# Later stores and a per-head copy: two small changes to a fused attention and MLP kernel

## The chip, the cores and the metric

The kernel runs on one core of a Trainium2 chip. The metric is the device time of one execution in microseconds, the median of several runs; lower is better. A profile of one execution goes with it: for every engine the instructions with start and duration, and for each wait what ended it. TensorE is called PE in the profile (PEld is its loading of weights), VectorE DVE, ScalarE ACT, GpSimd POOL, and the queue that issues most transfers SPq.

## The reference

Inputs are q, k, v of 8 batches, 8 heads, 576 positions and 64 columns in fp32, and the weights of an MLP (512 to 2048 to 512). Attention is of the Nyström kind: queries and keys are averaged over segments of 18 positions to 32 landmarks, three softmax matrices are made, and the inverse of the middle one is found by six Newton steps.

```python
A  = sm(q, k_lm)        # 576 x 32
Bm = sm(q_lm, k_lm)     # 32 x 32
C  = sm(q_lm, k)        # 32 x 576
Z = Bm.T / (norm1(Bm) * norminf(Bm) + 1e-6)
for _ in range(6):
    Z = 2 * Z - Z @ Bm @ Z
x = (A @ Z @ C @ v)     # then heads side by side: 8 x 576 x 512
# MLP
xn = (x - mean) / sqrt(var + 1e-6) * g_ln
out = x + relu(xn @ w_ch1) @ w_ch2
```

## The kernel before

The kernel interleaves two streams in one program. The attention works on sets of batches: (0), (1), (2), (3, 4), (5, 6), (7). A unit is half a batch, that is four heads whose 32 landmarks fill the 128 partitions; a set has W = 2 or 4 units. The MLP works on blocks of 128 rows, four blocks to a group, and is cut into small pieces (a generator) that fill TensorE while the attention waits for other engines. `fill(n)` takes n pieces. The order of instructions on each engine is thus fixed when the program is made.

In a Newton step the four heads of a unit are multiplied at once: `ebd` holds the four 32 x 32 matrices on the diagonal of a 128 x 128 operand, with zeros elsewhere. Before the change it is a product of the matrix, read four times over, with a mask of zeros and ones. The first set (batch 0) doesn't use it.

```python
def diagonal(name, src, W, mask):
    t = asm.tile([P, W, 4, LM], FP16, name=name, tag=name, bufs=1)
    dve.tensor_tensor(out=t[:], in0=src[:, :, None, :].broadcast_to([P, W, 4, LM]),
                      in1=mask, op=ALU.mult)
    return t

# one Newton step (attention2)
for it in range(6):
    psn = p1([P, W, LM + D], "psn")
    for w in range(W):
        MM(psn[:, w, lo:], ebd[:, w, :, :].rearrange("p a l -> p (a l)"), st[:, w, lo:])
    dve.scalar_tensor_tensor(out=stn[:, :, lo:], in0=st[:, :, lo:], scalar=2.0,
                             in1=psn[:, :, lo:], op0=ALU.mult, op1=ALU.subtract)
    st = stn
    if it < 5:
        ebd = diagonal("ebd", st[:, :, 0:LM], W, masks(W))
    else:
        bmbd = diagonal("bmbd", bm16, W, maskw...)
    ...   # scores of the queries in the first W // 2 steps
    yield
```

Beside this, GpSimd casts the incoming q, k and v to fp16 (`nat`, `natv`) and sums segments (`asum`, `s`); VectorE transposes them (`xT`), normalizes the attention's output into rows (`xblk`), and adds the MLP's result to them (`ot`). A finished block is centered (`xn`, mostly on GpSimd) and turned by a transposing transfer (`xnT`), which the MLP's first product `psh` reads. All of these transfers, the loads and the stores go through one queue, in order.

```python
def turn_by_dma(j):
    keep(nc.sync.dma_start(out=xnTs[g][:, :, ts(u, P)], in_=xn_of.pop(j)[:],
                           transpose=True))

# end of an MLP block
ot = mout.tile([P, DM], FP32, name="ot", tag="ot")          # 4 buffers
dve.scalar_tensor_tensor(out=ot[:], in0=pso[:], scalar=rstds[g][:, u:u + 1],
                         in1=x_blk.pop(j)[:], op0=ALU.mult, op1=ALU.add)
store(j, ot)                                                # two transfers
yield True

# the loop over an attention set
for step, _ in enumerate(attention2(c.bs, c)):
    fill(count[step])
    settle()              # centers finished blocks and issues their turns
    ...                   # next_cast, next_load, next_job
```

Of the kernel before, what the change touches and what calls it, by code (L numbers as in the profile page):

```python
# [9 lines left out]
FP16 = mybir.dt.float16  # L10
# [3 lines left out]
ALU = mybir.AluOpType  # L14
AX = mybir.AxisListType

P = 128
# [3 lines left out]
def kernel(  # L21
# [10 lines left out]
    nc = tc.nc  # L32
# [6 lines left out]
    LM = 32  # L39
# [12 lines left out]
        name=nc.get_next_instruction_name(), act_func_set_id=6, ins=[], outs=[]))  # L52

    const = ctx.enter_context(tc.tile_pool(name="const", bufs=1))
# [15 lines left out]
    dve, pool, scalar = Ordered(nc.vector), Ordered(nc.gpsimd), Ordered(nc.scalar)  # L70
# [75 lines left out]
    mask4 = const.tile([P, 4], FP32, name="mask4")  # L146
# [16 lines left out]


    maskw = const.tile([P, 4, 4], FP16, name="maskw")
    mask16 = const.tile([P, 4], FP16, name="mask16")
    nc.gpsimd.tensor_copy(out=mask16[:], in_=mask4[:])
    for w in range(4):
        nc.gpsimd.tensor_copy(out=maskw[:, w, :], in_=(mask4t if w % 2 else mask4)[:])

# [7 lines left out]
    for i in range(NV):  # L178
        t = const.tile([P, H // 2, NJ, D + 1], FP16, name=f"natv{i}")
# [3 lines left out]
    for i in range(NZ):  # L183
        t = const.tile([P, 4, D + 1], FP16, name=f"zcbd{i}")
# [77 lines left out]
    asm = ctx.enter_context(tc.tile_pool(name="asm", bufs=2))  # L262
# [16 lines left out]
            MM(idle[:, 0:cols], zeros[:], zeros[:, None, :].broadcast_to([P, cols // P, P]))  # L279


    def diagonal(name, src, W, mask):
        t = asm.tile([P, W, 4, LM], FP16, name=name, tag=name, bufs=1)
        dve.tensor_tensor(out=t[:], in0=src[:, :, None, :].broadcast_to([P, W, 4, LM]),
                          in1=mask, op=ALU.mult)
        return t

    def masks(W):
        return mask16[:, None, :, None].broadcast_to([P, W, 4, LM])


    def attention(bs):
        units = [(b, u) for b in bs for u in range(U)]
        W = len(units)
# [11 lines left out]
        for w, (b, u) in enumerate(units):  # L306
            for i, nm in enumerate(("q", "k")):
# [13 lines left out]
                t = aprep.tile([P, NJ, P], FP16, name="xT", tag="xT" + nm, bufs=5 if nm == "q" else 4)  # L321
# [14 lines left out]
            out=qbd[:],  # L336
            in0=pss[:, 0, :, :].rearrange("p u (e l) -> p (u e) l", e=2)[:, :, None, :]
            .broadcast_to([P, W * 2, 2, LM]),
            in1=mask2[:, None, :, None].broadcast_to([P, W * 2, 2, LM]), op=ALU.mult)
# [16 lines left out]
        bm16 = asm.tile([P, W, LM], FP16, name="bm16", tag="bm16")  # L356
# [22 lines left out]
        for w in range(W):  # L379
            for h in range(4):  # L380
# [4 lines left out]
                                op=ALU.max)  # L385
# [6 lines left out]
                                in1=cinv[:, :, None].broadcast_to([P, W, LM]),  # L392
                                op=ALU.mult)
        if not first:
            ebd = diagonal("ebd", st[:, :, 0:LM], W, masks(W))


        v_used.update(bs)
# [18 lines left out]
        for it in range(6):  # L417
            lo = 0 if it < 5 else LM
            psn = p1([P, W, LM + D], "psn")
            for w in range(W):  # L420
                if first:
                    for h in range(4):
                        sl = ds(32 * h, 32)
                        MM(psn[sl, w, lo:], st[sl, w, 0:LM], st[sl, w, lo:],
                           rb=32 * h, cb=32 * h)
                else:
                    MM(psn[:, w, lo:], ebd[:, w, :, :].rearrange("p a l -> p (a l)"),
                       st[:, w, lo:])
            stn = asm.tile([P, W, LM + D], FP16, name="st", tag="st")
            dve.scalar_tensor_tensor(out=stn[:, :, lo:], in0=st[:, :, lo:], scalar=2.0,  # L430
                                           in1=psn[:, :, lo:], op0=ALU.mult,
                                           op1=ALU.subtract)
            st = stn
            if not first and it < 5:
                ebd = diagonal("ebd", st[:, :, 0:LM], W, masks(W))
            if it < W:
                w = it
                psa = p2([P, NJ, 64], FP32, "psa")
                for (j0, j1) in ((0, 8), (8, NJ)):
                    for h in range(4):  # L440
                        r, e = divmod(h, 2)
                        rows = ds(64 * r, 64)
                        MM(psa[ds(32 * h, 32), j0:j1, :], klm[rows, w, ds(32 * e, 32)],
                           xT["q", w][rows, j0:j1, ds(64 * e, 64)], rb=64 * r, cb=32 * h)
                t = aexp.tile([P, NJ * 64], FP16, name="ea", tag="e")
                act(t[:], psa[:].rearrange("p j t -> p (j t)"), AF.Exp, scale=sc_A)
                ea.append(t)
            yield
# [156 lines left out]
    def attention2(bs, c):  # L605
# [39 lines left out]
        for w in range(W):  # L645
            for h in range(4):
# [9 lines left out]
        dve.tensor_tensor(out=st[:, :, 0:LM], in0=psse[:, 1, :, :],  # L656
                                in1=cinv[:, :, None].broadcast_to([P, W, LM]),
                                op=ALU.mult)
        ebd = diagonal("ebd", st[:, :, 0:LM], W, masks(W))


        pscv = ps2.tile([P, 2, 512], FP32, name="pscv", tag="p2")
        for y in range(W // 2):
# [13 lines left out]
            if y + 1 < W // 2:  # L677
                yield
        v_used.update(c.bs)
        pcv = pscv[:, :, 0:(W // 2) * (D + 1)].rearrange("p x (y e) -> p y x e", e=D + 1)  # L680
        rcv = asm.tile([P, W], FP32, name="rcv", tag="rcv")
        rcv_ = rcv[:].rearrange("p (y x) -> p y x", x=2)
# [9 lines left out]
        for it in range(6):  # L692
            lo = 0 if it < 5 else LM
# [3 lines that stand above are left out]
            stn = asm.tile([P, W, LM + D], FP16, name="st", tag="st")  # L697
            dve.scalar_tensor_tensor(out=stn[:, :, lo:], in0=st[:, :, lo:], scalar=2.0,
                                           in1=psn[:, :, lo:], op0=ALU.mult,
                                           op1=ALU.subtract)  # L700
            st = stn
            if it < 5:
                ebd = diagonal("ebd", st[:, :, 0:LM], W, masks(W))
            else:
                bmbd = diagonal("bmbd", bm16, W,
                                maskw[:, 0:W, :, None].broadcast_to([P, W, 4, LM]))
            if it < W // 2:
                for e in scores((2 * it, 2 * it + 1), lm["k"], xT, "q", sc_A, "ea"):
                    ea.append(e)
            yield  # L710
# [57 lines left out]
    def settle():  # L768
        while later:
            later.pop(0)()  # L770
# [50 lines left out]
    def store(j, ot, cols=ds(0, DM), queues=(nc.sync, nc.sync)):  # L821
        for i in range(2):
            b, c = divmod(2 * j + i, NJ)
            half = ot[ds(64 * i, 64), cols]
            if b < 2:
                queues[i].dma_start(
                    out=out[b].rearrange("(t j) f -> j t f", j=NJ)[c][:, cols], in_=half)
            else:
                queues[i].dma_start(
                    out=out[b].rearrange("(l c x) f -> c l x f", c=NJ, x=2)[c][:, :, cols],  # L830
                    in_=half)
# [44 lines left out]
    def mlp():  # L876
        for g in range(NGRP):
# [44 lines left out]
            for u in range(4):  # L922
                j = 4 * g + u
                if j == NBLK - 1:
                    last_block(j, hT)
                    return
                pso = psM.tile([P, DM], FP32, name="pso", tag="pm")
                for m in range(MCH):
                    MM(pso[:], hT[:, m, ts(u, P)], w2_16[:, m, :],
                       start=(m == 0), stop=(m == MCH - 1))  # L930
                    if m < MCH - 1:
                        yield True
                    if g == 0 and u >= 2 and m % 8 == 3:
                        n = len(turned.get(1, ()))
                        if 4 + n in xn_of:
                            transpose_block(1, n)
                            yield True
                ot = mout.tile([P, DM], FP32, name="ot", tag="ot")
                dve.scalar_tensor_tensor(out=ot[:], in0=pso[:], scalar=rstds[g][:, u:u + 1],
                                         in1=x_blk.pop(j)[:], op0=ALU.mult, op1=ALU.add)  # L940
                store(j, ot)
                yield True

    stream = mlp()

    def fill(n):
        for _ in range(n):
            if not next(stream, False):
                return


    a0, a1 = attention((0,)), attention((1,))
# [83 lines left out]
    for _ in range(6):  # L1036
        next_load()
    for i, _ in enumerate(a1):
        fill(5 if i < 9 else 7)
        settle()  # L1040
        next_cast()
        if 5 <= i < 11:
            sets[0].next_job()
# [7 lines left out]
              [14, 21, 21] + 6 * [10] + [10] + 5 * [9]]  # L1051
    for c, after, count in zip(sets, sets[1:] + [None], counts):
        for step, _ in enumerate(attention2(c.bs, c)):
            fill(count[step])
            settle()
            if late and step >= 3:
                late.pop(0)()
            if after and after.done < len(after.parts) and not (
                    after.k_by_pool and after.spread(step)):
                next_cast()  # L1060
            if after and step >= (5 if after.k_by_pool else 1):
                after.next_job()
        while after and (after.jobs or after.lms):
            fill(8)
            next_cast()
            after.next_job()
    for _ in stream:
        pass


# [28 lines left out]
```

The softmax here doesn't subtract the row's maximum and nothing guards it: scores larger than these inputs give would overflow.

## Time and profile before

| | |
|---|---|
| median of 3 runs | 329.57 us (328.33 to 330.2) |
| span of the profiled execution | 327.9 us |
| busy PE, DVE, ACT, POOL | 314.7, 175.7, 152.7, 153.3 us |
| ebd products on DVE | 30, 20.7 us |
| stores out of ot | 72 with the last ones, 2.4 us to landing |
| turns xnT by transfer | 28, 3.3 us to landing |

Busy time is the sum over the whole span, and the stages differ: POOL's work lies almost wholly in the first 160 us, that of PE everywhere. So what an engine costs is read from a stage, by the timeline and the waits, not from its total. A wait is put down to what ended it last. PE's ends are modelled, and part of its lost time is seen as waits of the weight load ahead of it (PEld), so the two lists overlap.

### The profile page before, as it was taken

The page shows a single profiled execution, that of the slowest core. Times are in us where ns is not written, and L with a number is a line of the kernel's source. Part 1 is how long each engine was busy: PE and PEld are TensorE (multiplying, and loading weights), DVE is VectorE, ACT ScalarE, POOL GpSimd, SP SyncE. Part 2 cuts the span into 40 slices and gives each one's busy share as a digit, 9 for nine tenths or more (in the row PEclk, how much of TensorE's full clock was granted, in tenths as well). Part 3 has the DMA queues.
Part 4 walks back from the last instruction along what each step waited for, and adds up shares of the span by engine and source line. Part 5 has one row for each costly group of instructions (what it writes and reads, how often), then busy time and mean ns, then how long its engine had stood idle before and what let it go on. Part 6 is the DMA issues. An engine that isn't in the chain of part 4 may idle for free.

```text
span 327.9 us, 8249 instructions
## 1 busy us (share of the span) xinstructions
PE 314.7 (96%) x3409; PEld 162.3 (50%) x3409; DVE 175.7 (54%) x395; ACT 152.7 (47%) x307; POOL 153.3 (47%) x241
## 2 busy tenths in 40 slices
PE   8889999999999999989999999999999999999995
PEld 8547864553445444435544445454444444444444
DVE  3668769779964797953237668722566120010012
ACT  3546762749960661957204672454046107305600
POOL 3389979999999999999800034100014000000000
PEclk9999999999999999999999999999999999999998
DMA  7999999898797864695022103330242126032023
GB/s 278 394 356 365 366 402 303 297 345 239 241 195 231 234 169 127 156 290 102 4 68 66 34 20 76 82 50 2 64 104 26 32 64 98 0 72 60 0 49 79
DMA packets 36397, 50.34 MB, mean 154 GB/s; under 512 B 17796, under 2 KB 22152, under 8 KB 36360
## 3 DMA queue, kind: packets, MB, share of 16 engines
q1 hardware_dynamic: 36200, 49.69, 52.7%
q8 instruction: 26, 0.43, 0.5%
q10 hardware_dynamic: 160, 0.13, 0.2%
q14 instruction: 11, 0.09, 0.1%
HBM read 36.70 MB, written 9.44 MB: 141 GB/s over the span
## 4 chain that ended last, share of the span: by engine, by line
PE 56%; POOL 22%; DMA 7%; issue 2%; ACT 2%; DVE 1%; SPq 0%; POOLq 0%
PE psh L74 26%; PE pso L74 25%; POOL asum L68 11%; POOL nat L68 6%; POOL natv L68 3%; DMA stg<-in_q_dram 3%; POOL xn L68 2%; DMA w2stg<-in_moe_w_ch_dram 2%; POOL s L68 1%; PE psy L74 1%; PE pscv L74 1%; DMA stg<-in_v_dram 1%; DMA stg<-in_k_dram 1%; DMA xnT<-xn 1%; ACT xn L68 1%
## 5 line engine op out<-in xcount | busy, mean ns | idle before, releaser
L74 PE MATMUL psh<-xnT,w 128*128 128x512 f16 (+1 forms) x640 | 133.7, 358 | 1.4 <-DMA xnT<-xn 1.4
L74 PE MATMUL pso<-w,hT 128*128 128x512 f16 (+1 forms) x592 | 132.9, 374 | 0.0
L68 ACT ACTIVATE hT<-psh 128x512 f16<-128x512 f32 x144 | 84.9, 597 | 97.6 <-PE psh L74 97.4
L74 PEld LDWEIGHTS <-w 128*128 128x128 f16 x640 | 59.5, 98 | 56.7 <-issue 3.1
L74 PEld LDWEIGHTS <-hT 128*128 128x128 f16 x592 | 56.1, 98 | 57.2 <-issue 0.8
L68 DVE SCALAR_TENSOR_TENSOR ot<-pso,rstd,xblk 128x512 f32<-128x512 f32 (+1 forms) x37 | 27.1, 732 | 77.6 <-PE pso L74 77.4
L68 POOL CAST nat<-stg 128x1152 f16<-128x1152 f32 x28 | 32.5, 1167 | 3.4 <-DMA stg<-in_k_dram 1.7
L68 POOL TENSOR_TENSOR asum<-asum 128x256 f32<-128x256 f32 (+2 forms) x54 | 28.4, 527 | 4.2
L68 DVE TENSOR_TENSOR xblk<-psy,rcpd 128x512 f32<-128x512 f32 (+1 forms) x40 | 27.6, 691 | 1.8 <-POOL w L68 0.2
L68 POOL TENSOR_TENSOR asum<-nat 128x576 f32<-128x576 f16 x18 | 23.4, 1299 | 1.5
L68 POOL TENSOR_SCALAR xn<-xblk,mvg 128x512 f16<-128x512 f32 x14 | 9.6, 694 | 30.9 <-ACT junk L68 30.9
L68 DVE SCALAR_TENSOR_TENSOR st<-st,psn 128x192 f16<-128x192 f16 (+3 forms) x36 | 14.2, 395 | 17.6 <-PE psn L74 17.4
L68 POOL CAST natv<-stg 128x1152 f16<-128x1152 f32 (+1 forms) x16 | 17.6, 1119 | 9.6 <-DMA stg<-in_v_dram 9.6
L68 POOL TENSOR_SCALAR negm<-mvg 128x1 f32<-128x1 f32 x14 | 2.7, 191 | 40.5 <-DVE mvg L68 35.9
L68 DVE TENSOR_TENSOR ebd<-st,mask 128x256 f16<-128x256 f16 (+1 forms) x30 | 20.7, 690 | 1.0
L68 DVE STREAM_TRANSPOSE xT<-nat 128x576 uint32<-128x576 uint32 x24 | 18.2, 760 | 2.2 <-POOL nat L68 2.2
L74 PE MATMUL psy<-zcbd,ea 128*128 128x260 f16 (+1 forms) x80 | 15.9, 276 | 1.0 <-DVE xblk L68 0.4
L68 ACT ACTIVATE ea<-psea 128x576 f16<-128x576 f32 x12 | 7.2, 648 | 16.5 <-PE psea L74 16.5
L74 PE MATMUL idle<-zeros 128*128 128x128 f16 (+2 forms) x82 | 13.4, 312 | 1.1 <-DVE eps_ln L172 1.1
L74 PEld LDWEIGHTS <-ea 128*128 128x128 f16 (+1 forms) x80 | 7.1, 100 | 12.2 <-issue 3.5
L68 ACT ACTIVATE junk<-xblk 128x512 f16<-128x512 f32 x14 | 8.8, 625 | 9.4 <-DVE xblk L68 9.2
L68 DVE BATCH_NORM_STATS2 st<-xblk 128x6 f32<-128x512 f32 x18 | 12.4, 688 | 0.5
(115 smaller groups left out, 263.0 us busy)
## 6 DMA issues: line engine op xcount, KB each, us to landing
stg<-in_q_dram SPq DMA_DIRECT2D x16, 576.0 KB, 6.0
stg<-in_k_dram SPq DMA_DIRECT2D x16, 576.0 KB, 5.7
out_dram<-ot SPq DMA_DIRECT2D x70, 128.0 KB, 2.4
stg<-in_v_dram SPq DMA_DIRECT2D x10, 576.0 KB, 6.4
w1stg<-in_moe_w_ch_dram SPq DMA_DIRECT2D x16, 256.0 KB, 6.0
w2stg<-in_moe_w_ch_dram SPq DMA_DIRECT2D x16, 256.0 KB, 5.2
stg<-in_v_dram SPq DMA_DIRECT2D x12, 288.0 KB, 5.5
xnT<-xn SPq DMA_TRANSPOSE x28, 3.3
```

Source lines behind the costliest of these rows:

```text
L68: return lambda *args, **kw: keep(getattr(self.engine, op)(*args, **kw))
L74: keep(nc.tensor.matmul(o, l, r, start=start, stop=stop, tile_position=(rb, cb), skip_group_check=(skip or cb != 0)))
```

## The change

It has two parts. The stores of a block are no longer queued when the block is done but one step later, after the turns that this step issues; at the end of the program, where no turns are left, they go out at once. This is to keep stores that wait for their data from standing ahead of turns in the queue. And `ebd` becomes one tile that is filled with zeros at the start, into which each Newton step copies only the four 32 x 32 pieces, one copy for each head, in place of a product over the whole operand. With it the operand `bmbd`, still a product, is made earlier, before the normalization of `pscv`.

```diff
-    mask16 = const.tile([P, 4], FP16, name="mask16")
-    nc.gpsimd.tensor_copy(out=mask16[:], in_=mask4[:])
+    ebd = const.tile([P, 4, 4, LM], FP16, name="ebd")
+    nc.gpsimd.memset(ebd[:], 0.0)
...
-    def diagonal(name, src, W, mask):
-        t = asm.tile([P, W, 4, LM], FP16, name=name, tag=name, bufs=1)
-        dve.tensor_tensor(out=t[:], in0=src[:, :, None, :].broadcast_to([P, W, 4, LM]),
-                          in1=mask, op=ALU.mult)
-        return t
+    def diagonal(src, W):
+        for h in range(4):
+            rows = ds(32 * h, 32)
+            dve.tensor_copy(out=ebd[rows, 0:W, h, :], in_=src[rows, :, :])
...                                        (attention2, before the Newton steps)
         v_used.update(c.bs)
+        bmbd = asm.tile([P, W, 4, LM], FP16, name="bmbd", tag="bmbd", bufs=1)
+        dve.tensor_tensor(out=bmbd[:], in0=bm16[:, :, None, :].broadcast_to([P, W, 4, LM]),
+                          in1=maskw[:, 0:W, :, None].broadcast_to([P, W, 4, LM]), op=ALU.mult)
...                                        (in the steps)
             if it < 5:
-                ebd = diagonal("ebd", st[:, :, 0:LM], W, masks(W))
-            else:
-                bmbd = diagonal("bmbd", bm16, W,
-                                maskw[:, 0:W, :, None].broadcast_to([P, W, 4, LM]))
+                diagonal(st[:, :, 0:LM], W)
...                                        (end of an MLP block)
-                store(j, ot)
+                if at_end:
+                    store(j, ot)
+                else:
+                    to_store.append((j, ot))
...
+    def work(n):
+        k = len(to_store)
+        fill(n)
+        settle()
+        for _ in range(k):
+            store(*to_store.pop(0))
...                                        (in the loops over the sets)
-            fill(count[step])
-            settle()
+            work(count[step])
```

More of the change, by code (lines that the diff above doesn't have):

```diff
@@ L279, in warm @@
             MM(idle[:, 0:cols], zeros[:], zeros[:, None, :].broadcast_to([P, cols // P, P]))
-    def diagonal(name, src, W, mask):
-        t = asm.tile([P, W, 4, LM], FP16, name=name, tag=name, bufs=1)
-        dve.tensor_tensor(out=t[:], in0=src[:, :, None, :].broadcast_to([P, W, 4, LM]),
-                          in1=mask, op=ALU.mult)
-        return t
-    def masks(W):
-        return mask16[:, None, :, None].broadcast_to([P, W, 4, LM])
+    def diagonal(src, W):
+        for h in range(4):
+            rows = ds(32 * h, 32)
+            dve.tensor_copy(out=ebd[rows, 0:W, h, :], in_=src[rows, :, :])
     def attention(bs):
@@ L434, in attention @@
             if not first and it < 5:
-                ebd = diagonal("ebd", st[:, :, 0:LM], W, masks(W))
+                diagonal(st[:, :, 0:LM], W)
             if it < W:
@@ L658, in attention2 @@
                                 op=ALU.mult)
-        ebd = diagonal("ebd", st[:, :, 0:LM], W, masks(W))
+        diagonal(st[:, :, 0:LM], W)
         pscv = ps2.tile([P, 2, 512], FP32, name="pscv", tag="p2")
@@ L702, in attention2 @@
             if it < 5:
-                ebd = diagonal("ebd", st[:, :, 0:LM], W, masks(W))
-            else:
-                bmbd = diagonal("bmbd", bm16, W,
-                                maskw[:, 0:W, :, None].broadcast_to([P, W, 4, LM]))
+                diagonal(st[:, :, 0:LM], W)
             if it < W // 2:
@@ L940, in mlp @@
                                          in1=x_blk.pop(j)[:], op0=ALU.mult, op1=ALU.add)
-                store(j, ot)
+                if at_end:
+                    store(j, ot)
+                else:
+                    to_store.append((j, ot))
                 yield True
     stream = mlp()
+    to_store, at_end = [], []
     def fill(n):
@@ L1038 @@
     for i, _ in enumerate(a1):
-        fill(5 if i < 9 else 7)
-        settle()
+        work(5 if i < 9 else 7)
         next_cast()
@@ L1053 @@
         for step, _ in enumerate(attention2(c.bs, c)):
-            fill(count[step])
-            settle()
+            work(count[step])
             if late and step >= 3:
@@ L1063 @@
         while after and (after.jobs or after.lms):
-            fill(8)
+            work(8)
             next_cast()
             after.next_job()
+    at_end.append(True)
     for _ in stream:
-        pass
+        while to_store:
+            store(*to_store.pop(0))
 _INS = ['q', 'k', 'v', 'moe_g_ln', 'moe_w_ch1', 'moe_w_ch2']
```

## The prediction

> **What bounds the kernel now.** I read the page from the top: engine shares, slices, the chain, then the waits of TensorE, then the timelines of single stretches. TensorE is busy in nearly every slice; POOL is as full until half way and then has nothing to do.
>
> ```profile
> PE   8889999999999999989999999999999999999995
> POOL 3389979999999999999800034100014000000000
> PE 56%; POOL 22%; DMA 7%; issue 2%; ACT 2%; DVE 1%; SPq 0%; POOLq 0%
> ```
>
> The chain runs through POOL from 42 to 138 us and from 141.7 us to the end through matmuls alone. From 150 us on TensorE has no gap, so nothing can be won there; a delay before that is paid in full, because TensorE's order is fixed and nothing behind it is slack. Busy TensorE is 314.7 of 327.9 us, so some 13 us are idle at all, of which about 4 are the tail and about 4 the start. The waits of TensorE (us in total, times, longest) name what the change touches; the third line is the weight load's view of partly the same moments as the first.
>
> ```profile
> PE psn L74 <- DVE ebd L68: 1.6, 3, 0.7
> PE psh L74 <- DMA xnT<-xn: 1.4, 1, 1.4
> PEld L74 <- DVE ebd L68: 4.4, 7, 1.2
> ```
>
> In the table by stretches (sum in us of PE, PEld, DVE, ACT, POOL) the first two are the Newton steps of the second and third attention set, the last those of the fourth:
>
> ```profile
> 66.00:82.00 16.00, 15.40 (x181) 7.14 (x178) 13.78 (x27) 11.34 (x26) 14.82 (x21) 1.00 0.92 293
> 98.00:124.00 26.00, 25.04 (x481) 12.40 (x480) 18.84 (x34) 11.40 (x21) 23.98 (x32) 1.00 0.74 204
> 170.00:185.00 15.00, 15.00 (x148) 7.36 (x147) 10.21 (x19) 7.13 (x12) 0.00 (x0) 1.00 0.32 72
> ```
>
> POOL fills over 90% of the first two and none of the last. That splits the 30 products ebd into two kinds. By form (busy us, mean ns):
>
> ```profile
> L68 DVE TENSOR_TENSOR ebd<-st,mask 128x512 f16<-128x512 f16 x12 | 10.8, 901 | 0.4
> L68 DVE TENSOR_TENSOR ebd<-st,mask 128x256 f16<-128x256 f16 x18 | 9.9, 548 | 0.6
> ```
>
> One by one in the timeline, with POOL idle they take 0.42 us (256 wide) and 0.69 us (512 wide) every time; with POOL busy 0.42 to 0.93 and 0.69 to 1.74. The longest, beside POOL's stream (start us, us):
>
> ```profile
> 118.58 1.74 DVE L68 TENSOR_TENSOR ebd<-st,mask 128x512 f16<-128x512 f16 x1
> 118.50 1.27 POOL L68 TENSOR_TENSOR asum<-nat 128x576 f32<-128x576 f16 x1
> 119.84 1.06 POOL L68 TENSOR_TENSOR asum<-asum 128x256 f32<-128x256 f32 x1
> ```
>
> POOL's sum ends at 119.77; ebd ends at 120.32, 0.55 later, which is its own data time (0.69 less about 0.16 of fixed time, the length of the smallest vector rows). So it stood still until POOL was through. POOL's next sum took 1.06 instead of its usual 0.74: it waited in turn.
>
> **What the Trainium skill says.** "SBUF — State Buffer", section "Who interferes with whom": VectorE and GpSimd share a port pair that is locked for a whole instruction; a VectorE instruction with two SBUF inputs or in a two-port mode must take it, and the loser blocks fully. The lines above agree. "VectorE: DVE Perf Modes", section "What auto-detection actually checks": a single-source 16-bit copy within SBUF whose outer counts are even takes the four-element mode, which uses both ports; a product of two tensors never does. So the new copies still need the lock, four times in place of once. The trace has a relative of theirs: the cast of 1152 elements to nat takes 0.76 us, about two elements per cycle. Same page, section "Two Vector instructions with no wait between them": an instruction that starts in another 32-partition quadrant than the one before starts only when all earlier ones have finished. The trace agrees:
>
> ```profile
> 52.84 0.69 DVE L68 TENSOR_TENSOR xblk<-psy,rcpd 64x512 f32<-64x512 f32 x1
> 53.56 0.75 DVE L68 SCALAR_TENSOR_TENSOR ot<-pso,rstd,xblk 128x512 f32<-128x512 f32 x1
> ...
> 57.32 0.69 DVE L68 TENSOR_TENSOR xblk<-psy,rcpd 128x512 f32<-128x512 f32 x1
> 57.92 0.74 DVE L68 SCALAR_TENSOR_TENSOR ot<-pso,rstd,xblk 128x512 f32<-128x512 f32 x1
> ```
>
> The first pair changes from rows 64 to 127 (batch 1 begins at row 64 of a block) to rows from 0: the second starts 0.03 us after the first's end. The other pair stays at row 0: it starts 0.09 us before. Each of the four copies begins in a new quadrant, so none overlaps.
>
> **The change, part by part.**
>
> *The copies, undisturbed.* A copy moves 64 elements per partition (128 for four units). Vector rows of 2 to 4 elements take 0.16 to 0.17 us; with four elements per cycle of the page's 0.96 GHz that makes, as an estimate, 0.18 and 0.20 us. Four in series with 0.03 between: 0.81 and 0.89 us, against 0.42 and 0.69. So where POOL is idle (sets from 170 us on, 11 of 30) ebd becomes 0.2 to 0.4 us longer, not shorter. There a step lasts over 2.2 us by the timeline and TensorE had no wait: cost 0.
>
> *The copies beside POOL.* Some 16 of the 30 lie before 160 us with POOL dense (19, less the three undisturbed ones named below). The question is how often POOL slips in between. A pair of two-port scalings of w1 in a row, beside a stream of POOL scalings that take 0.49 us each (24 in 11.74), shows it; alone one takes 0.34:
>
> ```profile
> 25.75 1.05 DVE L68 TENSOR_SCALAR w<-w1stg,g_sb 128x256 f16<-128x256 f32 x2
> 30.03 0.34 DVE L68 TENSOR_SCALAR w<-w1stg,g_sb 128x256 f16<-128x256 f32 x1
> ```
>
> The two advance one per POOL instruction (0.48 apart), each ending 0.15 after a POOL end. POOL instructions in the Newton steps come every 0.75 us or so (15 in 13 us from 110, but many of 0.32 to 0.74). If a small copy can follow another within a POOL gap, one extra wait falls on each ebd; if never, three. An extra wait costs about 0.6 us, since the copy's own fixed time lies inside it. I take two: 0.25 (first wait, as before) + 0.81 + 1.2 = about 2.3 us against a mean of 0.63 in the second set, and about 2.4 against 1.04 in the third: +1.6 and +1.4 us.
>
> *On the path.* A step is psn, st, ebd, psn. In the second set TensorE already waited for ebd in three steps of six, and 7 filling matmuls cover 1.5 us; I leave 0.3 of slack: 5 x 1.3 = 6.5 us. In the third, slack 0.4: 5 x 1.0 = 5. In the first set with ebd (40 to 49 us) POOL's w2 casts run until 45.4, every 0.68: 3 x 1.0, then 3 undisturbed steps without slack at 0.3: 4. Together 15.5 us. Back from that: while TensorE and VectorE stand, POOL runs dry for want of free buffers and leaves gaps for the copies; I take off 3.
>
> *bmbd.* Four products move from the last Newton step to the wait for pscv. Two waits of the weight load for bmbd, 0.7 us in all, go: -0.7.
>
> *The zeroed tile.* One fill of 512 elements at the start replaces a cast of 4. POOL has 7.4 us of idle time before its first natv cast: 0.
>
> *Stores behind the turns.* The queue works in order:
>
> ```profile
> 135.75 1.20 SPq L870 DMA_TRANSPOSE xnT<-xn  x1
> 137.04 1.24 SPq L829 DMA_DIRECT2D out_dram<-ot  x2
> 138.38 1.25 SPq L870 DMA_TRANSPOSE xnT<-xn  x1
> ```
>
> The third block was centered at 136.22 us, its turn issued at 138.38 behind two stores, and the psh that waits for it lost 1.42 us. In the new order one half store remains in between: 0.6 to 1.3 us saved, at most -1.4. Later the queue stands 80 us in sum at stores that wait for ot, but no TensorE wait follows there, so that is worth 0. And if the Newton steps run late, this wait shrinks by itself: the two don't add.
>
> Sum: 15.5 - 3 - 0.7 - 1.4 = +10.4 with two extra waits; with one it is, by the same terms, about +4; with three about +17; with none about 0 (+2.5 from the quadrant changes, -2.1 from the rest).
>
> **Rivals.** (a) *The copies are simply cheaper*: VectorE gains some us and the waits for ebd go. For it: the data time of the four together is 64 cycles against 256 (512 wide: 128 against 512), and POOL is held up less. Against it: the fixed time is paid four times, and the quadrant gaps. At best 325 to 327 us. (b) *The turn is the real wait* and the copies are neutral: 328 to 329 us. Against a larger gain: one TensorE wait of 1.42 us is all there is. (c) *VectorE becomes the bound* before 125 us: it is already 86% busy from 66 to 82 us and over 9 of 10 from 110 to 120, so waiting copies push back the transposes behind them and then POOL, which waits for free nat tiles: 345 to 350 us. (d) *One or two extra waits*: 333 to 340 us, my middle.
>
> **Range and chances.** I weigh no extra wait and rival (a) or (b) at a quarter, one at a quarter, two at 0.3, three and (c) at a fifth. The middle of that is 336.5 us, the range 328.5 to 348. Faster by over 2% (below 323) has no source in the trace: 0.03. Within 2% (to 336.2): 0.47. Slower: 0.50.
>
> **What would show it.** Right: groups of ebd copies whose mean is well over 0.2 us before 160 us and near it after; PE and PEld waits for ebd growing from 6 us to over 12, in the stretches 40 to 50, 66 to 82 and 98 to 124; no wait of psh for xnT. Wrong: copies that overlap, or four in a row between two POOL instructions; then the time stays near 328. It would also be wrong if VectorE's backlog starves TensorE of transposed keys, which I have only as rival (c).

## The result and the profile after

| | before | after |
|---|---|---|
| median of 6 runs | 329.64 us (328.33 to 330.2) | 341.76 us (341.36 to 344.7) |
| ratio after / before, of means | | 1.0394, 95% interval 1.0353 to 1.0435 |
| span of the profiled execution | 327.9 us | 340.0 us |
| VectorE for ebd | 20.7 us in 30 | 40.1 us in 120 |

The change makes the kernel 12 us slower. The page of the kernel after, first the slices of TensorE and POOL, then the chain by engine:

```profile
PE   8889879996699997899999999999999999999995
POOL 3489979999429999778960005400004100000000
PE 69%; DMA 11%; DVE 10%; POOL 6%; ACT 1%; issue 1%; SPq 1%; POOLq 0%
```

TensorE now has holes up to the 17th slice (8.5 us each, so to some 144 us), and VectorE, 1% of the chain before, carries 10% of it; behind the holes the row is full as before. The waits of TensorE and its weight load (us in total, times, longest):

```profile
PE psn L74 <- DVE ebd L68: 11.1, 9, 3.0
PEld L74 <- DVE ebd L68: 18.5, 16, 3.5
```

The two overlap, as before, where they stood at 1.6 and 4.4 us. By form on VectorE (busy us, mean ns | idle before us):

```profile
L68 DVE COPY ebd<-st 32x64 f16<-32x64 f16 x72 | 23.1, 321 | 1.3
L68 DVE COPY ebd<-st 32x128 f16<-32x128 f16 x48 | 17.0, 354 | 0.9
```

A copy takes 0.17 to 0.19 us when nothing disturbs it, so a mean of 0.32 and 0.35 hides two kinds. The timeline separates them. First a Newton step beside POOL, from VectorE, POOL and TensorE; then one at 191 us, where POOL is idle:

```profile
85.71 3.09 DVE L68 COPY ebd<-st 32x64 f16<-32x64 f16 x4
84.16 4.42 POOL L68 CAST natv<-stg 128x1152 f16<-128x1152 f32 x4
88.86 0.26 PE L74 MATMUL psn<-st,ebd 128*128 128x96 f16 x2 [3.00 <-DVE ebd L68]
191.21 0.78 DVE L68 COPY ebd<-st 32x128 f16<-32x128 f16 x4
```

The four copies lie under four casts that follow each other without a gap (4.42 us, 1.1 each). In the trace the first three copies take 0.71, 1.08 and 1.08 us: each ends 0.03 us after the end of one cast, and the next cast has begun by then. The fourth, with no cast left, takes 0.18. TensorE had 7 filling matmuls, 1.5 us in all, and then stood still for 3.00 us. At 191 us twice the data takes 0.78 us.

Where the 12 us arise shows in the start of the last `psn` of each of the first three sets that use ebd, and in the `psh` that waited for the turn (timeline of TensorE, us). The last two columns are experiments, told below.

| | before | after | late by | copies as tensor_scalar | copies as tensor_reduce |
|---|---|---|---|---|---|
| last psn, first set | 49.03 | 55.13 | 6.1 | 52.96 | 50.60 |
| last psn, second set | 80.32 | 92.66 | 12.3 | 91.02 | 83.64 |
| last psn, third set | 122.44 | 136.98 | 14.5 | 135.12 | 125.64 |
| psh behind the turn | 141.71 | 153.90 | 12.2 | | |
| span | 327.9 | 340.0 | 12.1 | 338.1 | 329.0 |

So the delay grows by 6.1, 6.2 and 2.2 us from one row to the next, 2.3 us come back before the next group of the MLP, and nothing happens after. The 2.3 us hold the wait of psh for xnT (1.42 us), which is gone: TensorE comes later than the turn.

### The profile page after: what moved, and what is told of

Same layout as the page of the kernel before. It is cut to its first block, busy times and chain, and to the rows that moved or that the text cites. A ratio compares the mean times of both kernels' runs of the same rounds, so it can differ in the third digit from the quotient of the medians.

```text
span 340.0 us, 8339 instructions
## 1 busy us (share of the span) xinstructions
PE 318.5 (94%) x3409; PEld 163.4 (48%) x3409; DVE 196.3 (58%) x485; ACT 153.0 (45%) x307; POOL 151.1 (44%) x241
## 4 chain that ended last, share of the span: by engine, by line
PE 69%; DMA 11%; DVE 10%; POOL 6%; ACT 1%; issue 1%; SPq 1%; POOLq 0%
PE pso L74 34%; PE psh L74 28%; DVE ebd L68 5%; DMA w1stg<-in_moe_w_ch_dram 4%; DMA stg<-in_v_dram 3%; POOL asum L68 3%; DMA stg<-in_q_dram 2%; PE psy L74 2%; PE pscv L74 2%; POOL nat L68 2%; DVE xT L68 2%; DMA w2stg<-in_moe_w_ch_dram 2%; DVE st L68 1%; PE psec L74 1%; ACT xn L68 1%
## 5 line engine op out<-in xcount | busy, mean ns | idle before, releaser
L74 PE MATMUL psh<-xnT,w 128*128 128x512 f16 (+1 forms) x640 | 135.4, 361 | 0.0
L74 PE MATMUL pso<-w,hT 128*128 128x512 f16 (+1 forms) x592 | 134.6, 377 | 0.0
L68 DVE COPY ebd<-st 32x64 f16<-32x64 f16 (+1 forms) x120 | 40.1, 334 | 2.3
L68 POOL TENSOR_TENSOR asum<-asum 128x256 f32<-128x256 f32 (+2 forms) x54 | 27.2, 503 | 4.2
L74 PE MATMUL psn<-st,ebd 128*128 128x96 f16 (+1 forms) x84 | 8.6, 209 | 13.4 <-DVE ebd L68 11.1
L74 PEld LDWEIGHTS <-ebd 128*128 128x128 f16 x84 | 5.7, 99 | 24.1 <-DVE ebd L68 18.5
```

The costliest lines, as they stand in the source:

```text
L68: return lambda *args, **kw: keep(getattr(self.engine, op)(*args, **kw))
L74: keep(nc.tensor.matmul(o, l, r, start=start, stop=stop, tile_position=(rb, cb), skip_group_check=(skip or cb != 0)))
```

## The experiments

Theory: the copies are slow because each must take the port that VectorE shares with GpSimd, and waits for GpSimd's instruction. Rivals: the order of the queue, the early bmbd, or four instructions in series with a change of quadrant each.

### Later stores alone

The kernel before with the stores of the change; ebd stays a product.

```diff
-                store(j, ot)
+                if at_end:
+                    store(j, ot)
+                else:
+                    to_store.append((j, ot))
```

(and `work` in place of `fill` and `settle`, as in the change)

> The kernel before with the later stores alone; ebd stays a product, bmbd stays late. Theory (the copies wait for GpSimd's port lock, the stores cost nothing): 328 to 329.5 us, the 1.42 us wait of psh for xnT shrinks to under 1 us. Rival (the new order of the queue delays loads or turns and carries the loss): 333 us or more, with new waits of GpSimd for stg.

Measured: 329.31 us against 329.64, ratio 0.9996 (0.9982 to 1.001): no difference. TensorE's list of waits:

```profile
PE psh L74 <- DMA xnT<-xn: 1.1, 1, 1.1
```

In the queue the third turn now goes out behind one half store instead of two, after the centering that it needs, and the wait is 1.1 us where it was 1.42, not under 1 us as expected. Even the 0.3 us can't be put down to the order of the stores: the change without the copies, below, has the same order and waits 1.4 us again,

```profile
PE psh L74 <- DMA xnT<-xn: 1.4, 1, 1.4
```

and the faster product, with the old order, waits 0.5 us. What sets this wait was not separated. The rival of a harmful order falls.

### Copies alone

The kernel before with the zeroed tile (its lines as in the change) and the four copies; stores and bmbd as before.

```diff
-    def diagonal(name, src, W, mask):
+    def diagonal(src, W):
+        for h in range(4):
+            rows = ds(32 * h, 32)
+            dve.tensor_copy(out=ebd[rows, 0:W, h, :], in_=src[rows, :, :])
...                                        (at each call)
-                ebd = diagonal("ebd", st[:, :, 0:LM], W, masks(W))
+                diagonal(st[:, :, 0:LM], W)
```

> The kernel before with the per-head copies alone; stores and bmbd as before. Theory (port lock): 341 to 344 us, 120 copies with a mean over 0.3 us, single copies of about 1.1 us beside GpSimd casts. Rival (the stores or bmbd matter): 335 us or less.

Measured: 343.34 us, ratio 1.0385 (1.0339 to 1.0431), the whole of the change's loss; the median counts one execution of 346.58 us at a clock of 0.973 that the ratio leaves out. By form (busy us, mean ns | idle before us), then the waits of psn:

```profile
L68 DVE COPY ebd<-st 32x64 f16<-32x64 f16 x72 | 23.6, 328 | 1.3
L68 DVE COPY ebd<-st 32x128 f16<-32x128 f16 x48 | 17.4, 363 | 0.9
PE psn L74 <- DVE ebd L68: 11.7, 12, 2.8
```

The longest single copy takes 1.175 us.

### The same copies by an instruction without a two-port mode

The kernel after, where a reduction over an axis of one element stands for the copy. The result is the same, the quadrants and the count too; only the instruction differs.

```diff
-            dve.tensor_copy(out=ebd[rows, 0:W, h, :], in_=src[rows, :, :])
+            dve.tensor_reduce(out=ebd[rows, 0:W, h, :], in_=src[rows, :, :, None],
+                              axis=AX.X, op=ALU.max)
```

> The kernel after, each of the four copies made as a tensor_reduce over an axis of one element: same quadrants, same data, same count, but one source, one element per cycle and no two-port mode. Theory (port lock): it doesn't wait for GpSimd; 0.23 us (64 elements) and 0.30 us (128) each, everywhere alike, four in series 1.0 and 1.3 us; time 328.5 to 332 us although each instruction is slower than an undisturbed copy. Rival (four instructions in series, each with its fixed time and its quadrant change, are the cost): 341 us or more, since the group is longer than the undisturbed copies.

Measured: 330.74 us, ratio 1.003 (1.0013 to 1.0047). By form (busy us, mean ns | idle before us):

```profile
L68 DVE TENSOR_REDUCE ebd<-st 32x64 f16<-32x64 f16 x72 | 15.2, 211 | 1.4
L68 DVE TENSOR_REDUCE ebd<-st 32x128 f16<-32x128 f16 x48 | 13.3, 277 | 0.9
```

And one step under POOL's casts, VectorE then POOL:

```profile
74.05 0.88 DVE L68 TENSOR_REDUCE ebd<-st 32x64 f16<-32x64 f16 x4
73.43 3.33 POOL L68 CAST nat<-stg 128x1152 f16<-128x1152 f32 x3
```

All 18 groups of the narrower form take 0.88 or 0.89 us and all 12 of the wider 1.15, beside POOL or not; the three casts take 3.33 us together, 1.15 each, and 27 of the 28 casts of this form in the run take 1.14 or 1.15. An instruction that is slower by itself (0.21 us against 0.17) wins back 11 of the 12 us. So neither four instructions in series nor the quadrants are the cost. What they do cost lies within the remaining 0.3%, of which the change without the copies, below, has 0.2% by itself; the waits of the weight load for ebd are 8.9 us against 4.4.

### Two-port instructions without a change of quadrant

The kernel after, where each piece is a multiplication of all 128 partitions with one column of the mask.

```diff
-            rows = ds(32 * h, 32)
-            dve.tensor_copy(out=ebd[rows, 0:W, h, :], in_=src[rows, :, :])
+            dve.tensor_scalar(out=ebd[:, 0:W, h, :], in0=src, scalar1=mask4[:, h:h + 1],
+                              scalar2=None, op0=ALU.mult)
```

> The kernel after, each copy replaced by a multiplication of all 128 partitions with one mask column (scalar per partition): still four instructions in two-port mode, 64 or 128 elements each, but all start at partition 0, so none is held for a change of quadrant. Theory in its plain form (each instruction takes the lock anew, GpSimd slips in between): still 336 to 343 us, with groups of over 1 us beside GpSimd. Rival (GpSimd slips in only because the quadrant change empties VectorE between copies): instructions start about 0.08 to 0.1 us apart, a group takes 0.5 us, time 327 to 331 us.

Measured: 340.89 us, ratio 1.0354 (1.0314 to 1.0395). A group beside POOL with POOL's two instructions, then an undisturbed one:

```profile
79.76 2.67 DVE L68 TENSOR_SCALAR ebd<-st,mask 128x64 f16<-128x64 f16 x4
79.90 1.14 POOL L68 CAST nat<-stg 128x1152 f16<-128x1152 f32 x1
81.12 1.27 POOL L68 TENSOR_TENSOR asum<-nat 128x576 f32<-128x576 f16 x1
...
235.33 0.68 DVE L68 TENSOR_SCALAR ebd<-st,mask 128x64 f16<-128x64 f16 x4
```

Undisturbed, the four overlap: in the trace they start 0.15 us apart with 0.24 each. Beside POOL the second takes 1.17 us, to the end of the cast (81.04), the fourth 1.29, to the end of the sum (82.39). So instructions that overlap are stretched to the end of GpSimd's as well: each waits anew, and a waiting GpSimd gets in between. The rival of the quadrants falls a second time.

### The change without the copies

The kernel after with one product per step, in the standing tile.

```diff
-        for h in range(4):
-            rows = ds(32 * h, 32)
-            dve.tensor_copy(out=ebd[rows, 0:W, h, :], in_=src[rows, :, :])
+        dve.tensor_tensor(out=ebd[:, 0:W, :, :],
+                          in0=src[:, :, None, :].broadcast_to([P, W, 4, LM]),
+                          in1=maskw[:, 0:1, :, None].broadcast_to([P, W, 4, LM]), op=ALU.mult)
```

> The kernel after with ebd made again by one masked product per Newton step (into the standing tile); later stores and early bmbd stay. Theory (only the copies cost): 328 to 329.5 us, within 0.5% of the kernel before. Rival (early bmbd or the standing tile add something of their own): over 331 us.

Measured: 330.04 us against 329.49, ratio 1.0018 (1.0005 to 1.0032): within 0.5%, though 0.5 us over the range expected. The copies are the loss. The early bmbd brings no gain that can be seen, and the trace shows where it can cost:

```profile
70.10 0.78 DVE L68 TENSOR_TENSOR bmbd<-bm,maskw 128x256 f16<-128x256 f16 x1
71.51 0.29 DVE L68 TENSOR_TENSOR st<-pscv,rcv 128x128 f16<-128x128 f32 x1
71.85 0.24 PE L74 MATMUL psn<-st,ebd 128*128 128x96 f16 x2 [0.43 <-DVE st L68]
```

In the second set bmbd now stands on VectorE ahead of the st that the first psn needs, and that psn waits 0.43 us; in the kernel before it doesn't wait there. The two waits of the weight load for bmbd (0.7 us) are gone in return. The difference in time is 0.55 us; no run takes bmbd alone, so that it is the cause is not shown.

### A faster product with one lock

The kernel before, with a mask whose last axis is stored instead of one column read 32 times.

```diff
-    mask16 = const.tile([P, 4], FP16, name="mask16")
-    nc.gpsimd.tensor_copy(out=mask16[:], in_=mask4[:])
...
     def masks(W):
-        return mask16[:, None, :, None].broadcast_to([P, W, 4, LM])
+        return bones[:, None, :, :].broadcast_to([P, W, 4, LM])
```

> The kernel before with one edit: the mask of the product is the existing 128 x 4 x 32 tile bones, whose last axis is stored out, in place of a mask column read 32 times over. Theory (VectorE takes two 16-bit elements per cycle when the innermost step of both inputs is one; one lock per step as before): 0.29 us (256) and 0.43 us (512) where GpSimd is idle, against 0.42 and 0.69; time 327 to 329 us, ratio 0.992 to 0.999. Rival (the read of st four times over keeps it at one element per cycle): durations and time unchanged.

Measured: 327.83 us, ratio 0.9934 (0.9909 to 0.996), a small gain on the kernel before. By form (busy us, mean ns | idle before us):

```profile
L68 DVE TENSOR_TENSOR ebd<-st,bones 128x512 f16<-128x512 f16 x12 | 8.0, 664 | 0.4
L68 DVE TENSOR_TENSOR ebd<-st,bones 128x256 f16<-128x256 f16 x18 | 7.3, 404 | 0.6
```

Undisturbed it takes 0.29 and 0.42 us in the trace, against 0.42 and 0.69; beside POOL it still waits (up to 1.27 us), once per step. "VectorE: DVE Perf Modes" of the Trainium skill, section "What auto-detection actually checks", states the condition, 16-bit tensors with an innermost step of one; the trace agrees: 256 more elements add 0.13 us here and 0.27 us in the kernel before. In TensorE's list psn waits 0.9 us for ebd, where it was 1.6, and psh 0.5 us for the turn, where it was 1.4; how the gain divides between the two wasn't separated.

### Everything that might help together

Later stores, early bmbd and this product.

```diff
-                          in1=maskw[:, 0:1, :, None].broadcast_to([P, W, 4, LM]), op=ALU.mult)
+                          in1=bones[:, None, :, :].broadcast_to([P, W, 4, LM]), op=ALU.mult)
```

(against the change without the copies)

> Later stores, early bmbd and the product with the stored-out mask together. Theory: the sum of the small gains, 326.5 to 328.5 us (ratio 0.990 to 0.998). Rival (TensorE's remaining waits are set by other work than ebd): no different from the kernel before.

Measured: 327.73 us, ratio 0.9945 (0.9928 to 0.9962). That is no better than the new mask alone, so no gain is seen from the other two.

## Why the prediction was right

It forecast 336.5 us with 328.5 to 348, and the time is 341.76. Step by step:

- **The bound and where it counts**: right. Before 150 us the delays are paid in full, after it the copies cost nothing: the lateness is 12.2 us at 153.90 and 12.1 at the end.
- **Undisturbed copies**: 0.81 and 0.89 us forecast for four, 0.73 and 0.78 measured. The premise of the quadrants held (starts 0.18 to 0.20 us apart, none overlapping), but it didn't matter for the result, as tensor_scalar shows.
- **Beside POOL**: the mechanism was right, the size a little high. Forecast 2.3 us per group in the second set and 2.4 in the third. Measured, as means of six in the trace: 1.66 (0.73 to 3.09) and 2.00 (1.39 to 2.81). The term behind it, two extra waits on every ebd, is too even: each long cast catches one copy, but between short sums two copies pass, and two groups in the second set met no POOL at all. POOL stood idle from 88.6 to 95.1 us:

```profile
95.11 0.69 POOL L68 TENSOR_SCALAR xn<-xblk,mvg 128x512 f16<-128x512 f32 x1 [6.54 <-ACT junk L68]
```

- **On the path**: forecast 4, 6.5 and 5 us for the three sets, measured 6.1, 6.2 and 2.2. In the first set the groups took 0.91 to 2.54 us where I had expected the last three undisturbed. That was a wrong reading of the kernel before, in which POOL is busy there too:

```profile
46.02 0.64 POOL L68 CAST w<-w2stg 128x512 f16<-128x512 f32 x1 [0.58 <-DMA w2stg<-in_moe_w_ch_dram]
47.55 1.15 POOL L68 CAST nat<-stg 128x1152 f16<-128x1152 f32 x1 [0.90 <-DMA stg<-in_k_dram]
48.97 1.15 POOL L68 CAST nat<-stg 128x1152 f16<-128x1152 f32 x1 [0.27 <-DVE ebd L68]
```

After the change such casts met two of the three groups. A step at half clock came on top (last section). In the third set the term that was too large is the copies' delay: the five groups between one psn and the next grew by 0.8 us each (from 5.3 to 9.2 us in sum), not by 1.4. From the first psn of the set to the last, 12.44 us became 15.62, so 3.2 of the 3.9 us were paid; the slack was less than the 0.4 us a step that I had allowed. Ahead of that set's first psn 1.0 us came back, which leaves the 2.2.
- **What comes back**: I took off 3 us for POOL's gaps and 2.1 for bmbd and the turn; 2.3 us came back between the third set and the next group, the turn's wait among them. For bmbd I had -0.7: the waits went, but no gain shows in the time. The sum of the middle case, +10.4, is nearest to the +12.1 us measured. Part of that fit is luck: the forecast was 2.1 us too low for the first set and 2.8 too high for the third, so the three sum to 15.5 against 14.5 measured. The cases of one and three extra waits are also wrong in their sums: 0.6 us on each of 13 groups is 7.8, which makes them +2.6 and +18.2 and not +4 and +17. The stated time was lower than the middle case because weight was given to cases in which the copies are harmless or nearly so; the run with the copies alone leaves the harmless ones no room.
- **The stores**: "at most -1.4" held as a bound, but the 0.6 to 1.3 us expected from them did not come: alone they leave the wait at 1.1 us, in another run with the same order it is 1.4, and nothing shows in the time. So this step, that the stores ahead of the turn set the wait, is not borne out.
- **Rivals**: (a) cheaper copies and (b) neutral copies fell. Of (c), that VectorE's backlog holds up others, a little is seen: psn waits 1.8 us in all for st, which stands behind copies or bmbd on VectorE, where it was 0.3. The starved transposes are not. (d), waits between the copies, is what happened, and the signs named for it came: waits for ebd in the three stretches, and none of psh for xnT.

## What to carry to other kernels

Splitting one VectorE instruction into several short ones moved fewer elements here, but the four took 0.73 us against 0.42 even undisturbed, and beside a full GpSimd each could wait for a whole instruction of it (3.09 us for four). Compare the same instruction's duration where GpSimd is idle and where it is busy: if they differ, as the 0.42 and 0.93 us of the product before did, count the instructions before the elements. Where pieces are needed, an instruction that doesn't wait for GpSimd can be the better one though it is slower by itself (330.74 us with tensor_reduce, 341.76 with copies). And a mask stored out along its last axis shortened the whole product from 0.42 to 0.29 us and from 0.69 to 0.42, with one wait per step as before.

## What was not expected of the hardware

In the profiled execution of the kernel after, TensorE's clock is halved from about 50 to 57 us, after it stood idle near 48 us (1.93 us in one wait). By stretches (sums for PE, PEld, DVE, ACT, POOL, then clock):

```profile
51.00:57.00 6.00, 5.31 (x21) 2.27 (x19) 5.29 (x12) 1.12 (x2) 5.52 (x8) 0.50 1.01 245
57.00:60.00 3.00, 3.00 (x22) 1.16 (x21) 2.40 (x6) 0.00 (x0) 2.69 (x6) 1.00 1.02 405
```

The kernel before shows no such stretch between its start and its tail. A later wait of 3.00 us in the same execution was not followed by one. With the copies alone there is one in another place, about a wait of 2.77 us that ends at 88.4 us:

```profile
88.00:91.40 3.40, 3.00 (x9) 1.19 (x10) 3.00 (x11) 0.66 (x2) 0.12 (x1) 0.50 0.91 318
```

The profiled execution with tensor_scalar has none and is 10.2 us longer than the kernel before all the same, so the clock adds to the loss but doesn't make it. How much it can add shows in the executions with the copies alone: 340.55 us at a mean clock of 0.999, 343.2 and 343.5 at about 0.99. What sets it off wasn't tried.
